# Batches 1 to 7 in two rounds over the halves of the features, the second round's second product by seven-for-eight twice, and the order of the work from a list scheduler

## The chip, the cores and the metric

The kernel runs on one core of one Trainium2 chip. The metric is the device time of one execution in microseconds (us). The kernel before has a median of 717.17 us over 3 runs (717.04 to 717.4). All of the arithmetic is in float32.

## The reference

```python
# x (8,8,512,64), state (8,8,32,64): batch, head, position, depth
scores  = scale * x @ state.T;  a  = softmax(scores)     # 512 x 32 per head
xread   = a @ state                                      # 512 x 64
scores2 = scale * state @ x.T;  a2 = softmax(scores2)    # 32 x 512
sread   = a2 @ x                                         # 32 x 64
tokens  = concat([xread, sread])        # per batch 512 + 32 rows of 8*64 = 512
h   = tokens @ w_in                     # (4352, 512) @ (512, 2048)
out = (h * erf(softplus(h))) @ w_out    # (4352, 2048) @ (2048, 512)
```

Attention is small. Nearly all of the work is the two products with `w_in` ("first product") and `w_out` ("second product"), and an activation between them. The 2048 columns of h are called the features.

## The kernel before

**Tiling.** The 512 tokens of a batch (`xread`) are handled together; the 32 rows of state (`sread`) of all eight batches are collected in `sT` and handled once, as 256 rows, at the end. The tokens are never formed: since xread = a · state, the state is first multiplied into `w_in` (`mixed_pair`, matmuls into PSUM and copies to `m`), and the first product is a · m. Batch 0 has a prologue of its own, ordered by a list of named steps (`start0`, `groups0`, `weights0`, `next0`); its last steps lie beside batch 1.

**Seven for eight.** Both products of batches 1 to 7 are made by a scheme in which a product of 2 x 2 blocks takes seven block products in place of eight, at the price of sums of blocks: sums of the weights (`combine_w` for `w_out`, once per half of the features), of the mixed states (`combine_m`), of the attention weights (`combine_a`), of the activation (`sums_of`), and of the results. `hidden_wide` is the first product (28 matmuls 256 wide for a half of the features of a batch, L489); it makes h in `ring`, and the softplus (L482) as it goes. `erf_part` and `finish_on_act` make the erf on ScalarE, `times_part` (L1127) multiplies by h on VectorE. `project_wide` is the second product (28 matmuls 256 wide for half of a unit's rows, L641).

**Loop.** The loop goes over 14 units: for each batch `b` of 1 to 7, `u` = 0 and 1, the two halves of the features. In each, the first product of all 512 rows is made, then `project_wide` twice (first two blocks of rows, then the other two, which are put off into the next unit as `pending`). The result of the first half is stored to the output by SP (`put_x`, L706), that of the second half is added to it in memory by a DMA that POOL issues (L704, 28 of them). The half of `w_in` that a unit does not hold is kept in DRAM (`kept_in`) and loaded again by `bring` (2 MB, L1108) every second unit. `w_out` and its sums T[1], T[2] and T[4] (in `raw`) stay in SBUF.

**Attention.** While batch b is worked on, the attention of batch b + 2 runs: `load_xq` (16 DMAs on SP, L104) and `load_x` (8 DMAs on SP, L75) load x in two layouts, `scores` (matmuls), then lists of steps on VectorE and ScalarE (`most`, `exps`, `total`, `ready`). `send` (L360) moves the token weights `xT` into `sc` by 16 DMAs on SP, and `read_tokens` (L275) multiplies them by x: this is the read.

**What sets the order.** The order is written out by hand. Each engine executes its own instructions in the order in which they were emitted, also in the region from the overlap on (`in_order`). `excursion` says where a unit makes the read, the mixed states and the scores; `add_jobs` and `fill` place small VectorE steps into the gaps of `hidden_wide` by a declared cost; `rest` places the others behind given steps of `project_wide`. Where 16 issues of DMAs stand on SP, whatever is emitted to SP after them waits behind them.

**End.** After batch 7 the state rows are made by `hidden_states` (L534, matmuls 128 wide), `project7` (L616 and L603) and `store7`, whose last step is two DMAs from SP and ScalarE.

Of the kernel before, what the change touches and what calls it, by code (L numbers as in the profile page):

```python
# [9 lines left out]
F32 = mybir.dt.float32  # L10
# [7 lines left out]
def kernel(  # L18
# [115 lines left out]
    kept_in = dram.tile([2, P, NF // 2, NK * P], F32, name="kept_in")  # L134
# [163 lines left out]
    reading = {}  # L298

    def attention(b, xT, *pool, held=None):  # L300
# [8 lines left out]
        d = {}  # L309
# [53 lines left out]
        def read():  # L363
            read_tokens(b, d["a2T"], d["z2"])
            if b + 1 < B:
                load_x(b + 1)

        reading[b] = read
        return list(most()), list(exps()), list(total()), list(ready())

    m_t = {}
# [18 lines left out]
    def combine_m(b, g):  # L390


        (X11, X12), (X21, X22) = ([m_t[b, 2 * g + j][:, e] for e in range(2)] for j in range(2))
        sx = mix.tile([P, 3, gw], F32, name="sx", bufs=2)
        S1, S2, S4 = (sx[:, k] for k in range(3))
        X[b, g] = X11, X12, S4, X22, S1, S2, X21
        tt = nc.vector.tensor_tensor
        return [lambda: tt(S1, X21, X22, op=ALU.add), lambda: tt(S2, S1, X11, op=ALU.subtract),
                lambda: tt(X21, X11, X21, op=ALU.subtract), lambda: tt(S4, X12, S2, op=ALU.subtract)]

    def combine_s(g):


        (X11, X12), (X21, X22) = ([of_group[2 * g + j][:, :, 2 * k:2 * k + 2, :]
                                   for k in range(2)] for j in range(2))
        S1, S2 = (mix.tile([P, GF, 2, P], F32, name="m") for _ in range(2))
        S4 = mix.tile([P, 3, gw], F32, name="sx", bufs=2)[:, 0:2].rearrange(
            "p i (j k f) -> p (i j) k f", j=2, k=2)
        tt = nc.vector.tensor_tensor
        X[B, g] = X11, X12, S4, X22, S1, S2, X21  # L410
        return [lambda: tt(S1, X21, X22, op=ALU.add), lambda: tt(S2, S1, X11, op=ALU.subtract),
                lambda: tt(X21, X11, X21, op=ALU.subtract), lambda: tt(S4, X12, S2, op=ALU.subtract)]

    def combine_a(b):

        if b < B:
            Y = aT[b].rearrange("p e (h r t) -> p e r h t", h=2, r=2)
        else:
            Y = sT.rearrange("p (e k) r n b -> p e r k (n b)", e=2)
        (Y11, Y12), (Y21, Y22) = ([Y[:, e, r] for r in range(2)] for e in range(2))  # L420
        sy = keep.tile([P, 3, 2, P], F32, name="sy", bufs=1)
# [12 lines left out]

    def hidden7(s, hs, product, view, between, copy=nc.scalar.copy):

        c11, c12, c21, c22 = (hs[k] for k in range(4))  # L440
        m1, u2, u3 = s[3], c12, c21

        def softplus(k):
            nc.scalar.activation(out=s[k], in_=hs[k], func=ACTF.Softplus)
        bank = lambda: ps_h.tile([P, S], F32, name="h")
        add = lambda o, x, y: nc.vector.tensor_tensor(o, x, y, op=ALU.add)
        p, q = bank(), bank()
        product(1, p)
        copy(m1, view(p))
        product(6, q)  # L450
        add(u2, m1, view(q))
        between()
        product(2, p, False)
        copy(c11, view(p))
        product(7, q, False)
        add(u3, m1, view(q))
        softplus(0)
        between()
        p, q = bank(), bank()
        product(5, p)  # L460
        add(c22, u3, view(p))
        product(4, q)
        add(c21, u3, view(q))
        between()
        marks[:] = product(3, p, False), add(c12, u2, view(p))
        for k in (3, 2, 1):
            softplus(k)

    def hidden_wide(b, g, low, between, fill, later):

        bank = lambda: ps_h.tile([P, S], F32, name="h")
        add = lambda o, x, y: nc.vector.tensor_tensor(o, x, y, op=ALU.add)  # L472
        view = lambda t: t.rearrange("p (h u) -> p h u", h=2)
        late = None
        for o in range(2):
            s, hs = ([ring[:, u, low:low + 2, k, 2 * o:2 * o + 2].rearrange(
                "p h i t -> p h (i t)") for k in range(4)] for u in range(2))
            c11, c12, c21, c22 = hs
            m1, u2, u3 = s[3], c12, c21

            def softplus(k, s=s, hs=hs):
                nc.scalar.activation(out=s[k], in_=hs[k], func=ACTF.Softplus)  # L482

            def product(n, bank, first=True):
                x, y = X[b, g][n - 1], Ys[b][n - 1]
                out = bank.rearrange("p (h i t) -> p i h t", h=2, i=2)
                for i in range(2):
                    q = P * (2 * o + i)
                    nc.tensor.matmul(out=out[:, i], lhsT=x[:, q:q + P], rhs=y,  # L489
                                     start=(first and i == 0), stop=(i == 1),  # L490
                                     skip_group_check=not first)

            p, q = bank(), bank()
            product(1, p)
            nc.scalar.copy(m1, view(p))
            if late:
                late(1)
            product(6, q)
            add(u2, m1, view(q))
            if o or not later:  # L500
                between()
            fill(1.8)
            product(2, p, False)
            nc.scalar.copy(c11, view(p))  # L504
            if not o and later:
                between()
            product(7, q, False)
            add(u3, m1, view(q))
            softplus(0)
            between()  # L510
            fill(1.2)
            p, q = (ps_at.tile([P, S], F32, name="at") for _ in range(2))
            product(5, p)
            add(c22, u3, view(p))
            product(4, q)
            softplus(3)
            add(c21, u3, view(q))
            between()
            fill(0.6 if o else 1.2)
            product(3, p, False)  # L520
            softplus(2)
            add(c12, u2, view(p))
            fill(0 if o else 1.2)
            late = softplus
        late(1)

    def hidden_states(g, n, between):
        s, hs = slot(n)

        def product(n, bank, first=True):  # L530
            x, y = X[B, g][n - 1], Ys[B][n - 1]
            for i in range(GF):
                for k in range(2):
                    last = nc.tensor.matmul(  # L534
                        out=bank[:, P * i:P * i + P],
                        lhsT=x[:, i, k], rhs=y[:, k],
                        start=(first and i == 0 and k == 0), stop=(i == GF - 1 and k == 1),
                        skip_group_check=not first)
            return last

        hidden7([s[:, k] for k in range(4)], [hs[:, k] for k in range(4)], product, lambda t: t,
                between)
        return s, hs

    def finish_on_act(s):
        nc.scalar.activation(out=s, in_=s, func=ACTF.Erf)  # L546

    def finish(s, hs, parts=(slice(0, GF),)):
        finish_on_act(s)
        for k in parts:  # L550
            nc.vector.tensor_tensor(s[:, k], s[:, k], hs[:, k], op=ALU.mult)

    def project(gT, g, acc, rs=range(NC), ts=range(GF)):
        for r in rs:
            for i in ts:
                nc.tensor.matmul(out=acc[r], lhsT=gT[:, i, P * r:P * r + P],
                                 rhs=w_out[:, GF * g + i, :],
                                 start=(g == 0 and i == 0),
                                 stop=(g == NG - 1 and i == GF - 1))
                yield  # L560

    def store(acc, put):
        for r in range(NC):
            ot = outs.tile([P, d_model], F32, name="ot", bufs=3)
            nc.scalar.copy(ot, acc[r])
            put(r, ot)
# [20 lines left out]
    def project7(gT, hs, g, first, last, acc, order=range(7)):  # L587


        blocks = lambda t: [t[:, k].rearrange("p (i t) -> p i t", i=GF) for k in range(4)]  # L590
        A11, A21, A12, A22 = blocks(gT)
        S1, S2, S3, S4 = blocks(hs)
        tt = nc.vector.tensor_tensor
        products = ((A12, B21, 0, 0), (A11, B11, 2, 0), (A22, T[4], 1, 0), (S2, T[2], 0, 1),
                    (S3, T[3], 2, 1), (S1, T[1], 1, 1), (S4, B22, 3, 0))
        for n, k in enumerate(order):
            lhs, rhs, bank, c = products[k]
            if last and n == 6:
                yield
                more = ps_at.tile([P, d_model], F32, name="at")  # L600
# [7 lines left out]
            for i in range(GF):  # L608
                if i % 2 == 0 and n:
                    yield  # L610
# [713 lines left out]
```

## Time and profile before

| | |
|---|---|
| median of 3 runs | 717.17 us |
| span of the profiled execution | 716.0 us |
| TensorE busy (matmul, PE) | 709.2 us, 4291 instructions |
| TensorE busy (weight load, PEld) | 562.4 us |
| VectorE busy (DVE) | 541.9 us, 880 instructions |
| ScalarE busy (ACT) | 378.9 us, 535 instructions |
| GpSimd busy (POOL) | 25.2 us, 34 instructions |
| DMA | 74.65 MB |

The profile is one execution. The time that it took is its span, 716.0 us; sums are made against that, and the runs' median lies 1.2 us above it. In the profile PE is TensorE's matmuls and PEld its weight loads, which lie beside them; DVE is VectorE, ACT ScalarE, POOL GpSimd and SP the engine that only issues DMAs. "L641" is a line of the kernel's code. `o<-w_out,ring` is output and inputs of an instruction by the program's names, then come the tiles' shapes, and x896 is how many there are. A busy time is not a time on the path that sets the end; the chain of waits (from the last instruction back to what released it) says which is.

### The profile page before, as it was taken

The page shows a single profiled execution, that of the slowest core. Times are in us where ns is not written, and L with a number is a line of the kernel's source. Part 1 is how long each engine was busy: PE and PEld are TensorE (multiplying, and loading weights), DVE is VectorE, ACT ScalarE, POOL GpSimd, SP SyncE. Part 2 cuts the span into 40 slices and gives each one's busy share as a digit, 9 for nine tenths or more (in the row PEclk, how much of TensorE's full clock was granted, in tenths as well). Part 3 has the DMA queues.
Part 4 walks back from the last instruction along what each step waited for, and adds up shares of the span by engine and source line. Part 5 has one row for each costly group of instructions (what it writes and reads, how often), then busy time and mean ns, then how long its engine had stood idle before and what let it go on. Part 6 is the DMA issues. An engine that isn't in the chain of part 4 may idle for free.

```text
span 716.0 us, 10962 instructions
## 1 busy us (share of the span) xinstructions
PE 709.2 (99%) x4291; PEld 562.4 (79%) x4291; DVE 541.9 (76%) x880; ACT 378.9 (53%) x535; POOL 25.2 (4%) x34
## 2 busy tenths in 40 slices
PE   8999999999999999999999999999999999999998
PEld 6444347688878878887888878887888888889997
DVE  6997888889868987698776877697777757665533
ACT  4999895647364526544455445562464535442340
POOL 0000000000100000000000000000000000000000
PEclk9999999999999999999999999999999999999999
DMA  8779686750358162514523280615242322002100
GB/s 257 236 209 251 210 243 180 169 159 31 52 98 205 28 140 40 161 37 106 80 41 138 58 148 1 177 31 144 34 120 70 95 41 27 33 29 30 25 7 30
DMA packets 144068, 74.65 MB, mean 104 GB/s; under 512 B 123024, under 2 KB 132624, under 8 KB 142480
## 3 DMA queue, kind: packets, MB, share of 16 engines
q1 hardware_dynamic: 139152, 65.89, 33.8%
q0 software_dynamic: 4032, 7.34, 7.6%
q8 instruction: 34, 0.56, 0.3%
q10 hardware_dynamic: 832, 0.72, 0.3%
q14 instruction: 18, 0.15, 0.1%
HBM read 49.81 MB, written 20.45 MB: 98 GB/s over the span
## 4 chain that ended last, share of the span: by engine, by line
PE 97%; DMA 2%; ACT 0%; SPq 0%; DVE 0%; issue 0%
PE o L641 48%; PE h L489 14%; PE at L489 10%; PE o L926 8%; PE h L534 3%; PE o L616 3%; PE at L919 2%; PE h L919 2%; PE h L383 2%; DMA raw<-in_moe_w_out_dram 2%; PE at L383 2%; PE at L275 1%; PE o L224 1%; DMA x<-in_x_dram 1%; PE at L908 1%; PE at L1018 0%
## 5 line engine op out<-in xcount | busy, mean ns | idle before, releaser
L641 PE MATMUL o<-w_out,ring 128*128 128x256 f32 x896 | 203.0, 379 | 0.0
L641 PEld LDWEIGHTS o<-w_out,ring 128*128 128x128 f32 x896 | 169.8, 190 | 24.9 <-DVE ring L1127 0.8
L641 PE MATMUL o<-raw,ring 128*128 128x256 f32 x672 | 161.4, 381 | 0.0
L641 PEld LDWEIGHTS o<-raw,ring 128*128 128x128 f32 x672 | 126.5, 190 | 25.9 <-ACT m L385 9.2
L482 ACT ACTIVATE ring<-ring 128x512 f32<-128x512 f32 x112 | 70.6, 631 | 59.8 <-DVE ring L472 59.2
L489 PE MATMUL h<-aT,m 128*128 128x256 f32 x336 | 81.9, 379 | 0.0
L1127 DVE TENSOR_TENSOR ring<-ring 128x1024 f32<-128x1024 f32 (+1 forms) x61 | 70.7, 1201 | 4.5 <-ACT ring L546 4.5
L489 PEld LDWEIGHTS h<-aT,m 128*128 128x128 f32 x336 | 63.8, 190 | 10.2 <-issue 0.9
L472 DVE TENSOR_TENSOR ring<-ring,at 128x512 f32<-128x512 f32 x84 | 57.2, 680 | 16.9 <-PE at L489 15.2
L926 PE MATMUL o<-w_out,ring 128*128 128x512 f32 x128 | 59.5, 599 | 0.0
L626 DVE TENSOR_TENSOR ot<-uv,o 128x256 f32<-128x256 f32 (+1 forms) x56 | 31.0, 553 | 30.1 <-PE o L641 28.1
L472 DVE TENSOR_TENSOR ring<-ring,h 128x512 f32<-128x512 f32 x56 | 38.0, 679 | 20.0 <-PE h L489 19.9
L664 ACT COPY ot<-o 128x256 f32<-128x256 f32 x28 | 10.4, 372 | 77.9 <-PE o L641 77.9
L704 POOL DMA_DIRECT2D out_dram<-ot x28 | 24.5, 946 | 652.1 <-DVE ot L626 574.8
L926 PEld LDWEIGHTS o<-w_out,ring 128*128 128x128 f32 x128 | 23.7, 190 | 28.1 <-issue 26.6
L626 DVE TENSOR_TENSOR ot<-ot,o 128x256 f32<-128x256 f32 x56 | 22.2, 417 | 27.9 <-ACT ot L664 27.7
L504 ACT COPY ring<-h 128x512 f32<-128x512 f32 x28 | 16.4, 586 | 47.9 <-PE h L489 47.9
L673 DVE TENSOR_TENSOR ring<-ring 128x512 f32<-128x512 f32 x56 | 38.6, 689 | 1.4
L674 DVE TENSOR_TENSOR ring<-ring 128x512 f32<-128x512 f32 x56 | 36.3, 685 | 0.0
L385 ACT COPY m<-h 128x512 f32<-128x512 f32 x13 | 7.6, 586 | 46.7 <-PE h L383 46.6
L546 ACT ACTIVATE ring<-ring 128x2048 f32<-128x2048 f32 x16 | 30.5, 1904 | 0.0
L489 PE MATMUL at<-sy,sx 128*128 128x256 f32 x112 | 28.7, 379 | 0.0
(203 smaller groups left out, 965.8 us busy)
## 6 DMA issues: line engine op xcount, KB each, us to landing
w_in<-kept_in SPq DMA_DIRECT2D x7, 2048.0 KB, 8.2
out_dram<-ot SPq DMA_DIRECT2D x33, 256.0 KB, 2.2
raw<-in_moe_w_in_dram SPq DMA_DIRECT2D x16, 512.0 KB, 5.4
raw<-in_moe_w_out_dram SPq DMA_DIRECT2D x8, 1024.0 KB, 5.9
xq<-in_x_dram SPq DMA_DIRECT2D x112, 64.0 KB, 3.2
x<-in_x_dram SPq DMA_DIRECT2D x56, 128.0 KB, 3.0
out_dram<-ot POOLq DMA_DIRECT2D x28, 256.0 KB, 4.5
sc<-xT SPq DMA_DIRECT2D x112, 32.0 KB, 1.9
```

Source lines behind the costliest of these rows:

```text
L383: nc.tensor.matmul(out=ps[k][e][q, :], lhsT=st[r, b, q], rhs=of_group[g][r, :, i, :], start=True, stop=True)
L472: add = lambda o, x, y: nc.vector.tensor_tensor(o, x, y, op=ALU.add)
L482: nc.scalar.activation(out=s[k], in_=hs[k], func=ACTF.Softplus)
L489: nc.tensor.matmul(out=out[:, i], lhsT=x[:, q:q + P], rhs=y, start=(first and i == 0), stop=(i == 1), skip_group_check=not first)
L546: nc.scalar.activation(out=s, in_=s, func=ACTF.Erf)
L626: add = lambda o, x, y: tt(o, x, y, op=ALU.add)
L641: nc.tensor.matmul(out=out, lhsT=lhs[:, i, :], rhs=rhs[:, g, i, :], start=(start and i == 0), stop=(i == GF - 1), skip_group_check=not start)
L673: return [lambda: tt(S1, A21, A22, op=ALU.add), lambda: tt(S2, S1, A11, op=ALU.subtract), lambda: tt(S3, A11, A21, op=ALU.subtract), lambd ...
L674: lambda: tt(S3, A11, A21, op=ALU.subtract), lambda: tt(S4, A12, S2, op=ALU.subtract)]
L919: nc.tensor.matmul(out=h_t[g, i], lhsT=m_t[0, g][:, e, P * i:P * i + P], rhs=aT[0][:, e], start=start, stop=not start)
L926: nc.tensor.matmul(out=acc[r], lhsT=gT[g][:, i, P * r:P * r + P], rhs=w_out[:, GF * g + i, :], start=(made_of[r] == 1), stop=(made_of[r] = ...
L1127: nc.vector.tensor_tensor(s[:, ks], s[:, ks], hs[:, ks], op=ALU.mult)
```

## The change

**Two rounds.** Batches 1 to 7 are all worked through for the first half of the features (round one, `u` = 0), with all of the attention in it; then the state rows, whole; then all batches for the second half (round two, `u` = 1). So `w_in` is loaded once, and the weights of a round stay. What the first product of round two needs of the attention (`aT` and its sums `sy`) is stored to DRAM as `kept_a` and `kept_y` in round one (`keep_y`) and loaded again (`bring_y`). `bring`, `hidden_wide`, `project_wide`, `project7`, `store7` and the POOL DMAs of `put_x` go.

**Products.** The first product keeps 28 matmuls 256 wide for a batch and half of the features. In round one the second product has 56 matmuls 256 wide for a batch, as before. In round two (`twice_product`) the scheme is applied twice, to blocks and to their quarters: 98 matmuls 128 wide take the place of 56 of 256. The quarter sums of the weights are made once (`sums_b`, 28 sums of 256 columns), those of the activation for each batch (4 groups of 4 sums); the results are seven tiles R1 to R7, some of which are added together (`total`) before seven DMAs from POOL for each batch, 49 in all, add them to the output. R3 and R6 go to the same rows and columns. The output of round one is put together in one tile, `oo`, and stored by SP.

**Intermediate sums in PSUM.** In `seven` (first product) and `second_product` a partial result that two results share is copied by ScalarE to a second PSUM bank, and later matmuls add to it there; before, VectorE added it to each result.

**Order.** Every step is declared by `op`: engine, cost in us, a time at which it is wanted, and the regions that it reads and writes; a DMA also has a time to land. `placed` simulates the engines with these costs and takes, for each engine, the step that can begin first, within a little slack the one that is due first; `emit` emits the steps in that order. A unit of round one is declared 40 us long, one of round two 34.5 us. `attend` declares the whole of `send` as 1.0 us on SP and 2.5 us to land, the loads of x as 1.0 and 4.0.

By the instructions of the two built kernels, 836 matmuls 256 wide on the second product and the state rows become 448, and 120 of 128 wide become 798; ScalarE has 758 instructions in place of 525, VectorE 837 in place of 882, POOL issues 49 DMAs in place of 28.

```diff
-    kept_in = dram.tile([2, P, NF // 2, NK * P], F32, name="kept_in")
+    kept_in = dram.tile([P, NF // 2, NK * P], F32, name="kept_in")
...
-    def hidden_wide(b, g, low, between, fill, later):
-    def project_wide(n, g, put, more):
-    def project7(gT, hs, g, first, last, acc, order=range(7)):
-    def store7(acc, put):
...
-            if more:
-                nc.gpsimd.dma_start(out=rows[2 * h + r][:, c], in_=ot[:, c], accum_op=ALU.add)
...
-    bring(1)
-    for n, (b, u) in enumerate((b, u) for b in range(1, B) for u in range(2)):
...
+    def op(engine, cost, at, go, reads=(), writes=(), table=None, land=0.0):
...
+    LAG = {PE: 0.3, ACT: 0.2, DVE: 0.2, SP: 0.2, GP: 0.2}
+    SLACK = {PE: 0.05, ACT: 0.2, DVE: 0.1, SP: 0.0, GP: 0.0}
+    LEAD = {PE: 99.0, ACT: 12.0, DVE: 12.0, SP: 30.0, GP: 30.0}
+    def placed(due, users):
...
+                first = min(max(free[e], t) for t in waiting.values())
+                n = min((k for k, t in waiting.items() if max(free[e], t) <= first + SLACK[e]),
+                        key=lambda k: (due[k] + (6.0 if ops[k][5] not in (None, loaded) else 0.0),
+                                       k))
...
+    def attend(b, at, scored_at, begun=False):
...
+            if b + 1 < B:
+                op(SP, 1.0, scored_at + 1, lambda: load_xq_static(b + 1),
+                   [], ["xq"] + ["xq%d" % i for i in range(NI)], land=4.0)
...
+            def send():
+                for m in range(NI):
+                    for i in range(NI):
+                        nc.sync.dma_start(out=rows[Ns * m:Ns * m + Ns, i],
+                                          in_=blocks[Ns * i:Ns * i + Ns, m])
+            op(SP, 1.0, at + 10, send, ["xT0", "xT1"], ["sc0", "sc1"], land=2.5)
...
+    def seven(product, regions, cost, names, s_of, at, apart, step):
+        p, q, r = names
+        mm(1, p, True, t)
+        op(ACT, 0.5, t, lambda: nc.scalar.copy(bank(q), bank(p)), [p], [q])
+        mm(5, r, True, t + step)
+        mm(2, p, False, t + 1.5 * step)
...
+    def oo():
+        return kept_tile("oo", lambda: outs.tile([P, 2, 2, d_model], F32, name="oo", bufs=1))
+    def second_product(b, u, splane, hplane, at, at_s):
...
+        def put(r, t):
+            op(SP, 0.1, t, lambda: nc.sync.dma_start(out=rows[r], in_=oo()[:, r]),
+               ["oo%d0" % r, "oo%d1" % r], [("out", b, r, c) for c in range(2)], land=4.0)
...
+    def twice_product(b, splane, hplane, inner, at, at_s):
+        for g, (ns, w, ks) in enumerate(GROUPS):
...
+                    for k, n in enumerate(ns):
+                        rhs = inner(n, m)
+                        for i in range(2):
+                            nc.tensor.matmul(
+                                out=out_[:, Q2 * k:Q2 * k + Q2], lhsT=lhs[:, k, i], rhs=rhs[:, i],
...
+        def put(g, x_, r, c, t):
+            op(GP, 1.0, t, lambda: nc.gpsimd.dma_start(
+                out=rows[r][:, :, E2 * c:E2 * c + E2], in_=results(g)[:, x_], accum_op=ALU.add),
+               every(g), [("out", b, r, c)], land=5.0)
...
+        put(*R3, 0, 1, t)
+        put(*R7, 1, 0, t)
+        put(*R5, 1, 1, t)
+        put(*R6, 0, 1, t + 1)
...
+    for b in range(1, B):
+        base = BASE + U * (b - 1)
+        def excursion(b, base):
+            read(b + 1, base + 3)
+            if b + 2 < B:
+                attend(b + 2, base + 18, base + 5)
+            turn_read(b + 1, base + 6)
+        def between(base, b=b):
+            if b + 1 < B:
+                mixed(b + 1, 0, base + (1 if b > 1 else -2))
+                if b > 1:
+                    excursion(b, base)
+                sums_y(b + 1, base + 8)
+                keep_y(b + 1, base + 12)
...
+        unit(b, 0, base, 1, hp[b], follow, between)
...
+    second_states(0, 0, base)
+    mixed(1, 1, base + 12)
+    second_states(1, 1, base + 22)
+    put_states(base + 30)
+    inner = sums_b(base + 20)
...
+        U = 34.5
+        unit(b, 1, base + 34.5 * (b - 1), 0, hq[b], follow, between)
+    emit()
```

## The prediction

> **What bounds the kernel now.** I read the page's first part, then the busy time by stretches, then the chain that ended last in order of time, then the timeline around the hand-over from batch 0 to batch 1.
>
> ```profile
> span 716.0 us, 10962 instructions
> PE 709.2 (99%) x4291; PEld 562.4 (79%) x4291; DVE 541.9 (76%) x880; ACT 378.9 (53%) x535; POOL 25.2 (4%) x34
> PE 97%; DMA 2%; ACT 0%; SPq 0%; DVE 0%; issue 0%
> ```
> ```profile
> 107.70:712.70 605.00, 604.97 (x3681) 511.84 (x3679) 452.23 (x747) 285.20 (x421) 24.54 (x28) 1.00 0.35 81
> ```
> From 107.7 to 712.7 us TensorE is busy for 604.97 of 605.00 us. Batches 1 to 7 and the state rows are one unbroken row of matmuls; nothing else has any say. So the change can win only matmul time, and every gap it makes in that row is a loss at full price. The own time of this execution is its span, 716.0; the median of the runs, 717.17, lies 1.2 above it.
>
> Two prices, from the chain in order of time (start, us, what):
> ```profile
> 241.60 12.09 PE o L641 x56
> 651.34 3.57 PE h L534 x32
> ```
> A float32 matmul leaves two records. 28 matmuls 256 wide in 12.09 us are 0.432 us each; 16 matmuls 128 wide in 3.57 us are 0.223 each, 3% over one half.
>
> The timeline where batch 1 begins (start, us, engine, line):
> ```profile
> 107.59 1.03 PE L489 MATMUL h<-aT,m 128*128 128x256 f32 x4
> 108.73 0.44 SPq L1108 DMA_DIRECT2D w_in<-kept_in  x1
> 110.65 1.30 DVE L351 STREAM_TRANSPOSE xT<-xT 128x512 f32<-128x512 f32 x2
> 112.01 13.40 SPq L360 DMA_DIRECT2D sc<-xT  x16
> 126.79 1.30 PEld L275 LDWEIGHTS at<-x,sc 128*32 128x32 f32 x64 [0.79 <-issue]
> ```
> and all issues of that line, ns min/median/max, with their way to landing:
> ```profile
> L360 SPq DMA_DIRECT2D sc<-xT x112: 586/608/1816, 112.0 to 559.1; - x112
> DMA to landing us min/median/max: 1.9/1.9/7.7
> ```
> The token weights reach the read (`read_tokens`) by 16 small DMAs on SP. They follow VectorE's two transposes. The last one started at 124.8 and the read at 126.8: even here the read began when the last piece had landed. At 0.608 us an issue, 16 need 15 x 0.608 + 1.9 = 11.0 us from the transposes to the read.
>
> The pitch of VectorE (timeline), and the DMAs of the line by which POOL adds to the output:
> ```profile
> 402.82 2.35 DVE L1127 TENSOR_TENSOR ring<-ring 128x1024 f32<-128x1024 f32 x2
> ```
> ```profile
> L704 POOL DMA_DIRECT2D out_dram<-ot x28: 865/865/1216, 183.9 to 677.1; - x28
> DMA to landing us min/median/max: 3.8/4.5/6.9
> ```
>
> **The change, part by part.** The orders of the built program give counts and places; durations are this trace's. Steps on VectorE are taken at their pitch: two L1127 of 1.22 in 2.35 us, so 1.14 for 1024 elements, 0.61 for 512, 0.335 for 256; a hand-over between engines 0.2 to 0.25.
>
> 1. Matmuls. 388 of 256 go (836 to 448), 678 of 128 come (120 to 798): -388 x 0.432 + 678 x 0.223 = -167.5 + 151.3 = **-16.3 us**. That is 56 x 0.432 = 24.2 against 98 x 0.223 = 21.9 in each of seven batches. All other matmuls stay in number and shape.
>
> 2. VectorE and ScalarE in the second round, per batch of 35.9 us of TensorE (21.9 + 28 x 0.432 + 1.9). VectorE: 4 products and 4 sums at 1.14, 4 additions to the first product and 4 sums of the mixed states at 0.61, 12 inner sums at 0.61 and 4 at 0.335, 8 additions to quarters (2.5 in all), 4 totals at 0.61: 27.6, 77%. ScalarE: 24, two thirds. Neither binds. From the last matmul of a first product to the second product that needs it lie addition, last softplus, table load (1.28), three of the erf (1.0 each), product: 8.4 us, behind 8.9 us of other matmuls. Costed at nothing; that cover has 0.5 us to spare, and if it went, each of 7 batches would pay.
>
> 3. The read of batch 1. Before, 19.2 us of matmuls stand between the first product's first matmul (107.6) and it. After, only 6.9: six pairs of 256 and two L926 matmuls. TensorE is there at 114.7, with 0.2 for a copy. The transposes end at 111.35, since one addition ahead of them is gone. The 2 MB load L1108, which made the 16 issues take 13.4 us, is gone too, so I take 11.0: 111.5 + 11.0 = 122.5. **+7.9** (0 if the pieces were landed in 3.5, as `attend` plans them; 12 with the 13.4 seen here).
>
> 4. Heads of batches 1, 2 and 3, where a second product waits for its activation. Batch 1: cover 3.0 us (score, mixed states, two transposes). Chain: 1.55 to the last softplus, 1.15 for the two copies of the scores, which stand ahead of the table load, 0.25 for a copy of the read, 1.3 and 1.0 for table and erf, 0.2 + 1.14 + 0.25; VectorE has five attention steps in its queue ahead of the product and ends at the same time: 6.9, so 3.9. Batch 2: cover 3.7, chain 5.4, so 1.7. Batch 3: the product is queued behind two sums of w_out (2.3), so 1.8. **+7.4** (0 to 10).
>
> 5. Batches 2 and 3 of the first round: attention of 3 and 4 within one batch. From the score of batch 3 to that of batch 4 TensorE has 10.4 us with the wait of step 4. VectorE's queue between them is 15.4 us of attention and products, and the x of batch 4 is transposed last in it: **+5.6**. The 16 pieces of batch 3 can only start after its transposes, 1.2 before that: + 11.0, with 2.9 us of matmuls in between: **+7.1** at the read of batch 3. The reads of 2 and 4 come 0.6 and 0.5 early. In all +13.8 (4 to 18). The vector steps queued behind the read of batch 3 (its scaling is in order) all move with it. From batch 5 the read stands some 10 us clear of its pieces.
>
> 6. Output of the first round. `oo` is one buffer; ScalarE's first copy of batch 3 waits until the rows of batch 2 are stored. The store stands on SP behind 8 loads of x and 16 of xq, 14 us of issues; ScalarE holds a copy that the first product needs: **+3.9** (0 to 8). In later batches the store stands ahead of xq: nothing.
>
> 7. Middle, and the rest: mixed states of round two with no matmul behind them (1.3 + 0.7 + 1.5), head of batch 4 (1.2): **+4.8** (2 to 12).
>
> 8. End. Before, 3.3 us lie between the last matmul (712.7) and the end. After: an addition (0.65), then POOL adds the result R3 to the output, and R6, which goes to the same rows, waits for that landing: 0.85 + 4.5 + 0.2 + 4.5 + 1.1 (from the last landing to the end, as before) = 11.1. **+7.8** (6 to 13). The other 47 such DMAs lie beside matmuls.
>
> At nothing: seven loads of w_in (2 MB each) go, `kept_a`/`kept_y` (0.9 MB, out and in, seven times) come, beside 40 us of matmuls each; the loads of round two have a whole batch to land.
>
> Sum: 716.0 - 16.3 + 7.9 + 7.4 + 13.8 + 3.9 + 4.8 + 7.8 = 745.3, as a median **746.5**.
>
> [...] In the trace TensorE never stands longer than 1.1 us while there is work, and its clock is granted in full throughout; so no row prices a longer gap. [...]
>
> **The rivals.** (a) Faster: the gaps of batches 1 to 3 (steps 3 to 6, 33.0) do not come, since the pieces land as the planner's 3.5 us has it and the chains are shorter than I added up. 716.0 - 16.3 + 4.8 + 7.8 = 712.3, median 713.5. It decides from the point where those four steps hold less than 3.7 us. For it: -16.3 is sure. Against: 16 issues at 0.608 are seen 112 times. (b) Transfers are hidden, vector chains are not: steps 3 and 6, and 8.2 of step 5, go: 726.5. For it: the landing alone is 1.9; against: it's the issue that takes long. (c) The second round is bound by VectorE and ScalarE: the 0.5 us cover of step 2 is missed by 2 us in each of seven batches, and the middle takes 12: 746.5 + 14 + 7 = 767. For it: VectorE at 77% in a fixed order; against: 0.5 us to spare. (d) The transfers are as slow as at 112 us, step 3 at 12 and the end at 13: 756.
>
> **How the numbers follow.** My sum 0.50, its own range 735 to 757; (a) 0.09; (b) 0.14; (c) 0.13; (d) 0.12; no difference that a measurement can tell (within 0.2%, 1.4 us) 0.02. The range 724 to 764 leaves out (a), no change, and part of (c). Faster 0.09, same 0.02, slower 0.89.
>
> **What the profile after would show.** Step 1: 1372 records of 128 wide on the inner product at some 275 ns. Step 3: an idle time of about 8 us on TensorE ahead of the read at 115 us, released by a DMA. Steps 4 to 6: TensorE busy clearly under 9 tenths in slices from 115 to 260 us and nowhere near that again before the middle. Step 8: some 11 us from the last matmul to the end, with POOL's two last DMAs. I'm wrong if those gaps are missing, or if TensorE has gaps in every batch of round two.

## The result and the profile after

The changed kernel takes 765.3 us (median of 4 runs, 764.7 to 767.7), the kernel before 717.1 in the same comparison: a ratio of 1.068, interval 1.0663 to 1.0693. The forecast was 746.5 with a range of 724 to 764. The direction was right, the size was too small by 18.8 us, and the time lies 1.3 us above the range.

The profiled execution has a span of 763.4 us, 47.4 above that of before. From the page: the span, the busy times, TensorE's busy tenths and its granted clock in 40 slices of 19.1 us, and the shares of the chain that ended last.

```profile
span 763.4 us, 12394 instructions
PE 713.5 (93%) x4871; PEld 571.4 (75%) x4871; DVE 536.9 (70%) x835; ACT 469.5 (61%) x770; POOL 60.2 (8%) x55
...
PE   8999995898599989999999999999999999999992
...
PEclk9999998999789999999999999999999999999997
...
PE 76%; DVE 10%; SPq 5%; issue 2%; ACT 2%; DMA 2%; POOL 0%; POOLq 0%; DVEq 0%; ACTq 0%
```

TensorE fell from 97% of the chain to 76%. The holes stand in the seventh to fifteenth slice, batches 1 to 4 of round one. From the sixteenth to the last but one there are none: round two never waits long for VectorE or ScalarE. The clock, full throughout before, now has dents at the two deepest holes.

The busy time from the first matmul of batch 1 to the last matmul, a stretch called the row below (us; TensorE's busy time comes first behind the length, the granted clock is the third number from the end):

```profile
107.20:749.20 642.00, 608.83 (x4261) 519.99 (x4259) 445.18 (x700) 375.92 (x656) 54.68 (x45) 0.98 0.39 80
```

642.0 us stand against 605.1 before (107.6 to 712.7). The 47.4 us are thus +36.9 in this row, +10.9 behind it (749.2 to 763.4 is 14.2, before 3.3), and -0.4 ahead of it. Within the row TensorE stands still for 33.2 us. TensorE's five largest waits (waiting line, what it waited for, us in total, times, longest):

```profile
PE at L1023 <- DMA sc<-xT: 14.3, 2, 8.8
PE o L1240 <- DVE ring L1197: 4.8, 4, 2.0
PE h L920 <- issue: 4.5, 1, 4.5
PE h L1160 <- ACT ring L1172: 3.0, 1, 3.0
PE at L1023 <- issue: 2.8, 2, 1.9
```

And the timeline at the read of batch 1 and at the stalled copy of batch 3 (start, us, engine, line):

```profile
111.08 10.56 SPq L360 DMA_DIRECT2D sc<-xT  x16
123.08 2.28 PE L1023 MATMUL at<-x,sc 128*32 128x64 f32 x64 [8.76 <-DMA sc<-xT]
```
```profile
266.42 0.43 SPq L1260 DMA_DIRECT2D out_dram<-oo  x1
269.39 0.59 ACT L1250 COPY oo<-o 128x512 f32<-128x512 f32 x1 [4.14 <-DMA out_dram<-oo]
271.22 1.13 PE L1160 MATMUL h<-sy,m 128*128 128x256 f32 x4 [3.04 <-ACT ring L1172]
```

The first shows the 16 issues on SP, then the read 1.4 us behind the last of them; it took 2.28 us for 64 matmuls that needed 1.44 in the read of batch 2 (at 176.6) and 1.43 in that of batch 4 (at 250.6). The second is the store of `oo` that ScalarE's copy waits for, and TensorE behind the copy.

The row's arithmetic: 605.1 - 16.3 of fewer matmuls is 588.8. On top come 33.2 of idle time. The trace grants half the clock for 6.8, 6.8, 6.8 and 3.4 us at the four longest gaps; TensorE worked 3.0, 4.5, 3.9 and 3.4 us in those, with records 256 wide 0.427 us apart in place of 0.216, so 7.4 of that was lost. What remains, 642.0 - 588.8 - 33.2 - 7.4 = **12.6 us, is lost with TensorE counted as busy**. The prediction had nothing for it.

The records of the single matmuls show where these 12.6 us lie. From the start of one record to that of the next are 0.216 us for a matmul 256 wide and 0.112 for one 128 wide, in this kernel as before, and summed over all such records this is 16.2 us less than before. On top come: 5.9 us since 88 of them follow their predecessor some 0.10 us late, where before 29 did; 3.1 at the 21 gaps, since idle time counts only from the end of a record, 0.38 us behind its start, where the next could have started after 0.216; 3.0 in the groups with small weights (64 x 32 and 128 x 32), the half clock left aside; and 0.5 that is spread. One such place: four matmuls take 0.71 us behind a small group and 0.61 elsewhere.

```profile
570.75 0.61 PE L1386 MATMUL o<-raw,ring 128*128 128x128 f32 x4
...
573.21 0.71 PE L1386 MATMUL o<-raw,w_in 128*128 128x128 f32 x4
```

### The profile page after: what moved, and what is told of

Its sections match the earlier page's. It is cut to its first block, busy times and chain, and to the rows that moved or that the text cites. A ratio compares the mean times of both kernels' runs of the same rounds, so it can differ in the third digit from the quotient of the medians.

```text
span 763.4 us, 12394 instructions
## 1 busy us (share of the span) xinstructions
PE 713.5 (93%) x4871; PEld 571.4 (75%) x4871; DVE 536.9 (70%) x835; ACT 469.5 (61%) x770; POOL 60.2 (8%) x55
## 4 chain that ended last, share of the span: by engine, by line
PE 76%; DVE 10%; SPq 5%; issue 2%; ACT 2%; DMA 2%; POOL 0%; POOLq 0%; DVEq 0%; ACTq 0%
PE o L1240 19%; PE o L1386 16%; PE h L1160 13%; PE o L630 7%; PE at L1160 6%; PE o L1563 3%; PE h L1514 2%; PE h L623 2%; PE at L623 2%; SPq L104 2%; PE at L1023 1%; DVE ring L1197 1%; SPq L1007 1%; DVE ring L1207 1%; SPq L990 1%
## 5 line engine op out<-in xcount | busy, mean ns | idle before, releaser
L1240 PE MATMUL o<-w_out,ring 128*128 128x256 f32 x448 | 105.6, 386 | 4.8 <-DVE ring L1197 4.8
L1172 ACT COPY ring<-h 128x512 f32<-128x512 f32 x112 | 65.0, 582 | 71.4 <-PE h L1160 71.2
L1240 PEld LDWEIGHTS o<-w_out,ring 128*128 128x128 f32 x448 | 85.1, 193 | 24.3 <-DVE ring L1197 7.7
L1197 DVE TENSOR_TENSOR ring<-ring 128x1024 f32<-128x1024 f32 x56 | 67.4, 1220 | 24.2 <-ACT ring L1194 24.1
L1240 PE MATMUL o<-raw,ring 128*128 128x256 f32 x336 | 81.9, 386 | 0.0
L1207 DVE TENSOR_TENSOR ring<-ring 128x1024 f32<-128x1024 f32 x56 | 67.6, 1220 | 0.2
L1386 PE MATMUL o<-w_out,w_in 128*128 128x128 f32 x448 | 60.5, 276 | 0.0
L1386 PEld LDWEIGHTS o<-w_out,w_in 128*128 128x128 f32 x448 | 56.8, 192 | 4.8 <-issue 3.4
L1194 ACT ACTIVATE ring<-ring 128x1024 f32<-128x1024 f32 x56 | 57.7, 1057 | 0.2
L1174 DVE TENSOR_TENSOR ring<-ring,at 128x512 f32<-128x512 f32 x28 | 19.1, 683 | 43.7 <-ACT ring L1172 43.7
L1178 DVE TENSOR_TENSOR ring<-ring,at 128x512 f32<-128x512 f32 x28 | 19.1, 683 | 41.6 <-PE at L1160 41.6
L1386 PE MATMUL o<-w_out,ring 128*128 128x128 f32 x336 | 45.6, 275 | 0.0
L630 PEld LDWEIGHTS o<-w_out,ring 128*128 128x128 f32 x128 | 23.7, 190 | 28.9 <-issue 27.6
L1386 PEld LDWEIGHTS o<-w_out,ring 128*128 128x128 f32 x336 | 42.4, 192 | 0.9 <-ACT oo L1396 0.2
L1386 PE MATMUL o<-raw,ring 128*128 128x128 f32 x252 | 34.9, 276 | 0.5 <-ACT sc L1396 0.5
```

The source lines that it names most:

```text
L630: nc.tensor.matmul(out=acc[r], lhsT=gT[g][:, i, P * r:P * r + P], rhs=w_out[:, GF * g + i, :], start=(made_of[r] == 1), stop=(made_of[r] = ...
L1172: op(ACT, 0.5, t, lambda: nc.scalar.copy(out_(), view(bank(name))), [name], w)
L1174: op(DVE, 0.6, t, lambda: tt(out_(), part(hplane, 2), view(bank(name)), op=ALU.add), [name] + area(hplane, ks=[2], os=[o]), w)
L1194: op(ACT, 0.97, at + n, lambda s_=s_: nc.scalar.activation(out=s_, in_=s_, func=ACTF.Erf), [], area(splane, ks=[k]) + ["soft", "erf"], tab ...
L1197: op(DVE, 1.14, at + n + 1, lambda s_=s_, h_=h_: tt(s_, s_, h_, op=ALU.mult), area(hplane, ks=[k]), area(splane, ks=[k]))
L1207: op(DVE, 1.14, at + k, lambda k=k, x_=x_, y_=y_, how=how: tt(get("h", k), get(*x_), get(*y_), op=how), area(v[x_[0]], ks=[x_[1]]) + area( ...
```

## The experiments

Two theories about the 47 us stood against each other. *Order*: the steps are sound, and the list scheduler's order, planned with wrong durations, makes the waits. *Substance*: two rounds and 98 pieces of 128 cost what their matmuls save, in any order. A third question was whether the half clock is a cost of its own. All runs are against the kernel before on the same chip.

| run | median us | ratio to before, interval |
|---|---|---|
| changed kernel | 765.3 | 1.068, 1.0663 to 1.0693 |
| e1_costs | 746.7 | 1.041, 1.0393 to 1.0428 |
| e2_warm | 765.5 | 1.067, 1.0651 to 1.0683 |
| e3_wide | 771.1 | 1.074, 1.0711 to 1.0775 |
| e4_tail | 762.0 | 1.062, 1.0603 to 1.0640 |
| e5_oopool | 760.8 | 1.061, 1.0590 to 1.0622 |
| e6_split | 755.0 | 1.053, 1.0513 to 1.0553 |
| e7_best | 743.7 | 1.036, 1.0349 to 1.0380 |
| e8_search | 721.0 | 1.005, 1.0034 to 1.0059 |
| e9_order | 722.9 | 1.007, 1.0059 to 1.0086 |
| e10_both | 714.9 | 0.996, 0.9952 to 0.9977 |
| e11_once | 727.5 | 1.014, 1.0125 to 1.0156 |

### The declared durations

```diff
-            op(SP, 1.0, at + 10, send, ["xT0", "xT1"], ["sc0", "sc1"], land=2.5)
+            op(SP, 9.7, at + 10, send, ["xT0", "xT1"], ["sc0", "sc1"], land=1.9)
...
-                op(SP, 1.0, scored_at + 1, lambda: load_xq_static(b + 1),
-                   [], ["xq"] + ["xq%d" % i for i in range(NI)], land=4.0)
+                op(SP, 9.6, scored_at + 1, lambda: load_xq_static(b + 1),
+                   [], ["xq"] + ["xq%d" % i for i in range(NI)], land=2.5)
...
-            op(SP, 1.0, at + 1, lambda: load_x_static(b + 1), [], ["x"], land=4.0)
+            op(SP, 4.3, at + 1, lambda: load_x_static(b + 1), [], ["x"], land=3.1)
```

> The changed kernel, but the scheduler is told what the trace shows for the DMAs of the attention: 9.7 us of SP for the 16 issues of send and 1.9 to land (declared: 1.0 and 2.5), 9.6 and 2.5 for the 16 loads of xq, 4.3 and 3.1 for the 8 of x (declared: 1.0 and 4.0). Nothing else is edited; the list order follows. Theory A (the gaps of batches 1 to 4 come from orders that were planned with DMAs ten times too cheap): the waits of the reads for sc (14.3 us), the 4.5 us ahead of the scores of batch 4 and about two thirds of the 7.4 us that work at half clock costs go: 763.4 - 14 - 5 = about 744, and TensorE waits no longer than 3 us anywhere before 300 us. Rival B (there is too little other work to put ahead, the chain of VectorE and ScalarE is the limit): the same waits come back at other lines, 757 to 763.

Measured 746.7, 18.6 less. In its trace the reads wait 1.0 us for `sc` in place of 14.3:

```profile
PE at L1023 <- DMA sc<-xT: 1.0, 1, 1.0
```

The idle time of the row is 17.6 us in place of 33.2, and no stretch of half clock is left before 190 us (the mean granted clock of the execution is 0.986 in place of 0.978). Theory A held within 3 us; what the planner believed of these DMA steps is worth 18.6 us. Waits of up to 3.2 us for VectorE (L1197, L1207) remained, 0.2 above what theory A allowed, so this isn't all of the order.

### The half clock

The edit also has such a loop, of 18 matmuls, ahead of the scores of batch 4.

```diff
...
             a2T, xt, sr = d["a2T"](), x_t[b], bank("at1")
+            for _ in range({1: 35, 3: 22}.get(b, 0)):
+                nc.tensor.matmul(out=sr[:, 0:P], lhsT=ident, rhs=ident, start=True, stop=True)
```

> The changed kernel in the same order, with spare 128-wide matmuls on constant data in front of three waiting groups, into the bank that the group overwrites next: 35 ahead of the read of batch 1 (7.8 us of an 8.8 us wait), 18 ahead of the scores of batch 4 (4.0 of 4.5), 22 ahead of the read of batch 3 (4.9 of 5.5). They take away the standing still and leave the waits. Theory A (the half clock after a gap is a cost of its own): no half clock before 260 us; 3.0 us of work after the read of batch 1 and 3.9 after that of batch 3 ran at half clock, so 1.5 + 1.95 = 3.4 us less, 760; what was lost after the scores of batch 4 was lost inside the wait for the next read and brings nothing. Rival B (the recorded clock costs nothing): 763.4. Rival C (the spare matmuls delay what follows): over 764.

Measured 765.5: no gain. By stretches of the changed kernel, then of this run (same columns as above):

```profile
120.00:125.00 5.00, 1.93 (x63) 1.96 (x64) 0.00 (x0) 0.00 (x0) 0.00 (x0) 0.50 0.61 210
125.00:130.00 5.00, 5.00 (x27) 3.53 (x19) 2.31 (x5) 3.14 (x6) 0.00 (x0) 0.89 0.67 151
```
```profile
120.00:125.00 5.00, 4.04 (x86) 3.73 (x85) 0.00 (x0) 0.00 (x0) 0.00 (x0) 1.00 0.62 210
125.00:130.00 5.00, 5.00 (x21) 3.66 (x20) 3.57 (x6) 3.38 (x7) 0.00 (x0) 1.00 0.79 180
175.00:180.00 5.00, 3.26 (x67) 2.94 (x68) 1.64 (x4) 0.00 (x0) 0.00 (x0) 0.71 0.51 155
```

The clock was indeed full behind the read of batch 1, and batch 1's second product began 1.3 us earlier (143.0 for 144.3). But the read of batch 2 then waited 2.4 us in place of 1.0, because its pieces on SP came no sooner, and that longer wait brought a half clock of its own (0.71 in the third line), as did a wait of 3.1 us that stayed at the read of batch 3. By the scores of batch 4 the kernel was 1.7 us later than without the spare matmuls. So the half clock is real work lost, but ahead of a read that waits for SP it is paid in waiting anyway. Rival B's number came out, but not for its reason: the local gain was there and didn't arrive. (In the profiled execution the row is 1.3 us longer and the end 1.0 shorter.)

### The issues on SP

```diff
+                        queue = nc.gpsimd if (NI * m + i) % 3 == 1 else nc.sync
-                        nc.sync.dma_start(out=rows[Ns * m:Ns * m + Ns, i],
+                        queue.dma_start(out=rows[Ns * m:Ns * m + Ns, i],
```

> The changed kernel with 5 of the 16 DMAs of every send issued by POOL and 11 by SP, in the changed kernel's order otherwise. Theory A (the reads wait for the issues, 0.62 to 0.67 us each on SP, and not for what is moved): the last of 11 is issued 6.8 us after the transposes in place of 10.6, POOL's five take 4.3 to 6 (0.87 to 1.2 each, as its DMAs to the output do), so the reads of batches 1 and 3, which wait 8.8 and 5.5 us for sc, start some 3.5 us sooner each: 765.3 - 7 = 758. Rival B (the data's way is the limit: pieces of 128 bytes): no difference. Rival C (five such DMAs cost POOL much more than those to the output): slower than 766.

Measured 755.0, 10.3 less where 7 was expected. In the profiled execution 8.6 of it lie in the row; 2.0 lie at the end, whose code is the same. Its timeline at the read of batch 1:

```profile
111.06 7.30 SPq L361 DMA_DIRECT2D sc<-xT  x11
111.75 3.08 POOL L361 DMA_DIRECT2D sc<-xT  x5 [110.44 <-PE h L1162]
119.72 2.38 PE L1025 MATMUL at<-x,sc 128*32 128x64 f32 x64 [5.43 <-DMA sc<-xT]
```

The read starts 3.4 us sooner, as expected; that of batch 3 6.7 us sooner (204.2 for 210.9), since the scores ahead of it came sooner too. The reads waited for issues and not for data. POOL issued these at 0.62 us each, and SP its eleven at 0.66.

### The store of the first round

```diff
-            op(SP, 0.1, t, lambda: nc.sync.dma_start(out=rows[r], in_=oo()[:, r]),
+            op(GP, 1.2, t, lambda: nc.gpsimd.dma_start(out=rows[r], in_=oo()[:, r]),
```

> The changed kernel with the two stores of a batch in round one issued by POOL, which has nothing else to do then, in place of SP, where they stand behind the loads of x. Theory A (step 6: the copy of batch 3 that ScalarE holds waits for a store that stands behind 16 loads of xq): the wait of 3.0 us at 268 us and the half clock after it (1.7) go, 765.3 - 4.7 = 760.6, and the four stores that come before it land sooner. Rival B (the store only hid another wait, the copy is late for its input too): under 1.5 us gained, 764 or more.

Measured 760.8, 4.5 less where 4.7 was expected. The 3.0 us wait and the half clock behind it are gone from its trace. The read before them now waits 2.4 us and has a half clock of 3.4 us instead (half from 252.3). Step 6's mechanism is confirmed. That the total came out so near is luck: in the profiled execution the row is 2.9 us shorter, and the other 2.2 lie at the end, which the edit does not touch (12.0 in place of 14.2).

### The end

```diff
+        if last:
+            groups[3:] = [(3, slice(0, 1), (7,), "h", slice(2, 3)),
+                          (3, slice(1, 2), (3,), "h", slice(3, 4))]
...
+            total(R1, R6, R5, t + 1)
+            put(*R1, 0, 1, t + 1)
...
+            put(*R3, 0, 1, t + 6)
```

> The changed kernel with another end: in batch 7 of round two alone the last group of the second product is split in two (product 7, then product 3), the sum of R1, R5 and R6 goes into R1's tile and is put as soon as R5 and R6 are there, R7 and R5 follow while product 3 runs, and R3 is put last with nothing else to wait for. Before that edit 14.2 us lie between the last matmul (749.2) and the end (763.4). Theory A (the end is a chain of two POOL DMAs on the same rows): 0.6 + 1.2 + 4.7 + 1.3 = 8 us remain, 757. Rival B (three POOL DMAs that land side by side slow each other, 7.4 us for the last against 4.6 alone): 760.

Before this edit, and after it (timeline of POOL at the end):

```profile
750.17 2.44 POOL L1425 DMA_DIRECT2D out_dram<-sc  x2 [8.83 <-DVE sc L1401]
752.17 1.68 POOL L1425 DMA_DIRECT2D out_dram<-m  x1
754.75 1.20 POOL L1425 DMA_DIRECT2D out_dram<-m  x1 [0.91 <-DMA out_dram<-sc]
```
```profile
751.08 1.20 POOL L1432 DMA_DIRECT2D out_dram<-sc  x1 [2.16 <-DVE sc L1438]
751.82 1.71 POOL L1432 DMA_DIRECT2D out_dram<-m  x1
753.34 1.42 POOL L1432 DMA_DIRECT2D out_dram<-sc  x1
```

The fourth DMA, which waited for the landing of another, is gone; from the last matmul to the end are 9.3 us in place of 14.2 (752.5 to 761.8). The median fell by 3.3 only: in the profiled execution the row is 3.3 us longer, with gaps of nearly the same lengths in the first batches but 30.7 us of half clock in place of 23.9 (mean granted clock 0.977 in place of 0.978, both with the half clock behind the last matmul); why is open. In the changed kernel the slowest of the 49 DMAs took 7.4 us from issue to landing and the median one 4.7, and from the last issue to the end are 8.7 us: rival B had a part of it.

### The second round alone

```diff
-        if u == 0:
-            second_product(b, u, splane, hplane, base, at_s)
-        else:
-            twice_product(b, splane, hplane, inner, base, at_s)
+        second_product(b, u, splane, hplane, base, at_s)
```

> The changed kernel with the second product of round two done as in round one (seven for eight once, 56 matmuls 256 wide for a batch in place of 98 of 128; no sums of weight quarters; two DMAs from POOL for a batch in place of seven; 37.5 us declared for a batch in place of 34.5). Two rounds, list order and intermediate sums in PSUM stay. Theory A (the 128-wide scheme gives what its matmuls save): a batch of round two takes 24.2 + 12.1 + 2.1 = 38.4 us in place of 36.7 measured, 7 x 1.7 = 12 slower, the end some 5 us shorter and the middle 1 shorter: 763.4 + 12 - 6 = 769. Rival B (hand-overs eat the 128-wide gain, a batch of round two stays at 36.7 to 37): 758 to 760.

Measured 771.1, 5.8 more than the changed kernel. The start of the first group of mixed states in two successive batches of round two gives a batch's time; the changed kernel, then this run:

```profile
572.19 1.09 PE L1061 MATMUL h<-x,st 64*32 64x512 f32 x16
...
608.85 1.09 PE L1061 MATMUL h<-x,st 64*32 64x512 f32 x16
```
```profile
575.95 1.09 PE L1061 MATMUL h<-x,st 64*32 64x512 f32 x16
...
614.29 1.09 PE L1061 MATMUL h<-x,st 64*32 64x512 f32 x16
```

36.7 us with 128 wide, 38.3 with 256: 1.7 us for a batch, where the matmuls alone are 2.3 (step 1). And with 41.0 for a batch of round one in both, two rounds with seven-for-eight once take 79.3 us for a batch, against 78.55 of the kernel before: so the two rounds cost 0.75 us for a batch, of the 1.7 that the 128-wide scheme gains.

### The small groups side by side

The edit declares a batch's two groups of mixed states as one step, on top of e1's durations and e4's end.

```diff
+        op(PE, 1.9, at, together, ["w_in%d%d" % (u, j) for j in range(2)], ["h0", "h1", "at0", "at1"])
...
-            op(PE, 0.9, at, on_pe, ["w_in%d%d" % (u, j)], names)
+            order.append(on_pe)
```

> Three edits together on the changed kernel: the DMA costs as the trace shows them (the run with 746.7), the split end (14.3 to 9.3 us behind the last matmul), and the two groups of matmuls for a batch's mixed states declared as one step, so that they stand side by side as in the kernel before. Theory A (small groups that stand apart cost TensorE about 0.2 us each time, with no idle time shown): a batch of round two goes from 36.66 to 36.3 and the whole to 746.7 - 4.9 - 2 = 740. Rival B (a joint step needs four PSUM banks free at once and waits for them): a batch of round two of 36.7 or more, 742 or more in all. In any case the theory that the 128-wide scheme can't win back its two rounds says that it stays above 717.

Measured 743.7. Two successive batches of round two:

```profile
560.80 1.09 PE L1068 MATMUL h<-x,st 64*32 64x512 f32 x16
561.68 1.06 PE L1068 MATMUL at<-xq,st 64*32 64x512 f32 x16
...
596.86 1.09 PE L1068 MATMUL h<-x,st 64*32 64x512 f32 x16
```

A batch takes 36.06 us, 0.6 less than with the groups apart (36.66 in the changed kernel and in e1), and none of these shows an idle time there. So one turn to a small group and back, saved, is worth 0.6 us that no idle time tells. In the middle rival B was right: two waits of 2.0 and 2.6 us with half clocks behind them (the mean granted clock is 0.983, in e1 0.986). In the profiled execution the row is 3.4 us longer than e1's (626.0 for 622.6) and the end 4.4 shorter, which is why the total gained 3 and not 7.

### The order alone

The steps stay as they are; a list of their numbers takes the place of the scheduler's. It was found by moving single steps, never ahead of what they depend on, with the durations of the traces, until TensorE's waits were short.

```diff
-        for n in order:
...
+        for n in ORDER:
             ops[n][3]()
```

> The changed kernel with every step as it is, and only the order in which the steps are emitted replaced: in place of the list scheduler's, an order found by moving single steps (none ahead of what it depends on), with durations as the traces show them, until TensorE's waits are short. Theory A (the waits and the half clock are made by the order alone): from 107.3 us on the row takes 605.0 - 16.3 of matmuls and the 12.3 that the small hand-overs cost without idle time, so the last matmul ends at about 708 and the end, unchanged, is 14.3 later: 722, 724 as a median. Rival B (the transfers and the chains of VectorE and ScalarE at the heads of batches 1 to 4 can't be covered in any order): over 10 us of idle time stay between 107 us and the last matmul, 735 or more.

Measured 722.9, 42.4 less with the same steps. TensorE's slices, and the stretch from the first matmul of batch 1 to the last matmul:

```profile
PE   8999999999999999999999999999999999999992
```
```profile
107.20:706.60 599.40, 597.24 (x4261) 512.44 (x4259) 444.79 (x700) 365.43 (x654) 54.09 (x45) 1.00 0.41 85
```

2.2 us of idle time are left, the clock is full. Theory A expected 724; rival B is out. This is also the cleanest price of the change: its row is 599.4 where matmuls alone say 588.8, so 8.4 us are lost besides, with TensorE counted as busy: 5.1 more than before by late starts (82 of them), 1.0 at its six gaps, 1.9 in the small groups, the rest spread. Two more runs take the two halves of the change apart.

> Round two with the second product by seven for eight once (as in the run with 771.1), with an order found as for the run with 722.9 and all of its DMAs on SP. With the waits gone on both sides this prices the two changes apart. Theory A (the 128-wide scheme is worth 1.68 us for a batch, as the batches of round two showed, and the two rounds cost some): 722.9 + 7 x 1.68 = 734.7, less 5.9 for the shorter end and some 1 for the middle: 727 to 729, so two rounds without the 128-wide scheme lose some 10 us to the kernel before. Rival B (the gain of 128 wide came from better-filled gaps): 722 or less.

This run (the edit of e3 and an order of the same kind) measured 727.5, inside its 727 to 729. Spans: before 716.0, two rounds with the scheme once 725.5, with the scheme twice 720.8, the list scheduler's order 763.4. So two rounds cost 9.5 (4.9 in the row, 5.0 at the end, which takes 8.3 us in place of 3.3, less 0.4 ahead of the row), the 128-wide scheme gives 4.7 back (10.6 in the row, less an end of 14.2 in place of 8.3), and **the order costs 42.6**. The first two prices hold for orders found by such a search; another order can shift them.

### A version that beats both

> An order found in the same way, with two more edits: the DMAs of the attention (16 of send, 16 and 8 of x) go half to SP and half to POOL, and the end of the last batch is split as before. Theory A: 708 at the last matmul as in the run beside it, and 9.3 behind it: 717.5, a median of 718 to 719, level with the kernel before. If the hand-overs without idle time shrink with the order too (the small groups side by side): down to 712. Rival B (the waits come back): 727 or more.

Measured 721.0. In this run the order had the two transposes ahead of batch 1's send the other way round. In the trace one of them starts only at 118.1, behind the send (110.6 to 116.2) and a wait of VectorE of 7.5 us: by the code half of that batch's token weights went out untransposed, so this is not the time of the same computation. The next run holds that pair in its order; both have the split end and share the attention's DMAs between SP and POOL:

```diff
+                        queue = (nc.sync, nc.gpsimd)[i % 2]
+                        queue.dma_start(out=rows[Ns * m:Ns * m + Ns, i],
...
-        load_xq(b)
...
+                (nc.sync, nc.gpsimd)[k].dma_start(
```

> The run with half of the attention's DMAs on POOL and the split end, with a new order. In the run with 721.0 the two transposes that stand ahead of batch 1's send had changed places, so that half of batch 1's token weights were sent before they were transposed and VectorE stood 7.5 us behind the send (4.95 us of TensorE); that pair is now held in its order. Theory A: without that wait and the half clock behind it (1.2) the last matmul ends at 704 to 706 in place of 710, the end is 8.6 behind it: 713 to 715 of span, a median of 714 to 716, 0.2 to 0.4 percent faster than the kernel before. Rival B: another wait of the first batches takes its place, 718 or more.

```profile
107.40:703.30 595.90, 594.40 (x4261) 513.54 (x4259) 447.87 (x709) 366.71 (x659) 132.71 (x167) 1.00 0.41 87
```

Measured 714.9 against 717.4: a ratio of 0.996, interval 0.9952 to 0.9977. Its row is 595.9 us with 1.5 idle, 9.2 shorter than that of before; the end (703.3 to 713.5, 10.2) takes 6.9 of that back. Of the 12.6 us lost in busy time 5.6 are left: 3.3 by late starts, 1.0 at gaps, 1.0 in the small groups.

## Why the prediction failed

The sum of the span, 745.3, missed by 18.1 us: 12.6 that step 1 put at nothing, 7.4 of half clock that the sum left out and 3.1 by which step 8 was too small, less 4.6 by which steps 3 to 7 were too large and 0.4 ahead of the row.

- **Step 1** failed. The counts and the price of a matmul were right (1372 records of 128 wide, 276 ns in the mean where 275 were expected), but "all other matmuls stay in number and shape" was taken to mean that nothing is lost between them. A batch of the two rounds takes 77.65 us against 78.55 before, so the steady gain is 0.9 and not 2.3. The 12.6 us are the largest miss. They shrink with the order (12.6, then 8.4 in e9 and 5.6 in e10, which also moves DMAs and splits the end), so most of them belong to how the pieces follow one another: late starts, gaps and small groups.
- **The clock** has no term in the sum, because no row of before showed a long gap: TensorE's longest wait was 1.1 us there, at a granted clock of 1.00. In the trace after, 7.4 us are lost at half clock, at gaps of 3.0 to 8.8 us. That belongs in the sum, though e2 (765.5 for 765.3) shows that taking away part of it wins nothing while the reads wait for SP.
- **Step 8** was undersized: 10.9 in place of 7.8. The chain was the right one; from the last issue (754.75) to the end are 8.7 us, where the sum had 4.5 for the landing and 1.1 behind it, 5.6. The sum also leaves out the addition of 0.65 that it names first.
- **Steps 3 to 7** held in place and mechanism and were 4.6 too high in sum (33.2 of 37.8). Step 3: 8.8 for 7.9. Step 4: 2.5 at batch 1, 1.2 and 1.0 at batches 2 and 3, 4.7 for 7.4. Step 5: 4.5 for the scores, 5.5 for the read of batch 3 (2.3 more were hidden in the half clock ahead of it), 1.0 and 1.9 for the reads of batches 2 and 4, 12.9 for 13.8; for the scores it had 5.6, where its own 15.4 less 10.4 is 5.0. Step 6: 3.0 for 3.9. Step 7: 2.6 for 4.8. The last 1.1 lie in the last batch.
- **Step 2** was right: no head of a batch in round two waits for its activation.

Sum by the measured sizes: 716.0 - 16.3 + 33.2 + 7.4 + 12.6 + 10.9 - 0.4 = 763.4. Of the rivals, (a) and (b) fell with the 16 issues, which are slow as the trace of before had shown; (c) fell with step 2; (d) was nearest on the end, and on that alone. The range failed because its upper rivals each had one further delay, while here two terms that the sum left out came together: the clock, which comes with the gaps, and the 12.6 us, of which 8.4 stay in e9 with hardly a gap.

## What to carry to other kernels

When an order comes from a planner, compare its declared durations with issue times in a trace first: here three kinds of steps that were declared at 1.0 us of a queue and took 4 to 10 cost 18.6 us, and the order as a whole 42.6, nine times what the 128-wide scheme wins. A kernel whose bound engine is busy for 99% has no slack to pay for new hand-overs from one group of matmuls to another: price a count of matmuls by a whole batch's period, small groups included, and not by matmuls times their pitch. And a gain that is accounted in front of a wait for something else does not arrive.

## What the runs showed of the hardware

- In the changed kernel the granted clock was half for 6.83 us from 119.25, from 197.76 and from 208.00, and for 3.41 us from 272.85. The first three stretches began inside gaps of TensorE of 8.76 us (114.32 to 123.08), 4.52 (195.52 to 200.04) and 5.51 (205.40 to 210.92), the fourth 1.6 us behind the end of one of 3.04 (268.18 to 271.22). The next longest gaps, 1.98 us (142.33 to 144.31) and 1.87 (248.68 to 250.55), lie in stretches of full clock (126.08 to 197.76, 214.82 to 272.85). In e2 the clock was 0.71 from 175 to 180 us, at the wait of 2.4 us of the read of batch 2. What decides whether the half clock follows a gap is open.
- In e6 POOL issued five pieces of `sc` in 3.08 us, 0.62 each, and SP eleven in 7.30, 0.66 each. A DMA from POOL that adds to the output took 1.20 us in the median in the changed kernel (14 of `oo`), 0.87 in the kernel before (28 of `ot`).
- With the same code at its end the time from the last matmul to the end was 14.2, 14.2, 13.7, 13.2, 12.2 and 12.0 us in six kernels; why is open. Why a matmul follows some 0.10 us late at the places counted above is open too.
